# Another written-out order for five passes, and one instruction for the copy of the keys out of PSUM

## The chip, the cores and the metric

The kernel runs on one core of a Trainium2 chip. The time is the device time of one launch in microseconds; the median of three runs is given. One execution was also profiled; all rows below come from it.

## The reference

The program is a chunked attention followed by a two-layer network on its result, `x`:

```
# q, k, v: (4, 8, 768, 64); mem_k, mem_v: (4, 8, 8, 64)
for c in range(768 // 32):                       # chunks of 32 queries
    keys = concat(mem_k, k[..., c0 - 16 : c0 + 32 + 8])   # cut at both ends
    a = softmax(q[..., c0 : c0 + 32] @ keys.T / 8)
    out[..., c0 : c0 + 32] = a @ concat(mem_v, v[same rows])
x = out as (3072 tokens, 512)
h = x @ w_in                                     # w_in: (512, 2048)
g = h + sin(alpha * h) ** 2 / (alpha + 1e-9)
result = g @ w_out                               # w_out: (2048, 512), result float32
```

## The kernel before

**Tiling.** Each of the four batches has 768 tokens. Attention takes 96 queries at a time against 128 key rows (a window of the keys with the 8 memory keys in it), so a batch has 8 blocks `j`, numbered 0 to 7; the first batch is cut by pairs of heads and halves instead. The first matrix product of a batch makes 16 tiles `ft` of 128 features by 768 tokens, in two halves of 384; each half is four matmuls (L426), so a tile is eight matmuls and takes two of PSUM's eight banks. The second product is 6 x 16 matmuls of 512 columns per batch (L464).

**Passes.** The opening pass prepares constants and does the attention of batch 0. Pass `i` (0 to 3) then does both matrix products of batch `i` and, between the matmuls of the second one, the attention of batch `i + 1`. So passes 0, 1 and 2 hold attention, and pass 3 only products. In a pass, TensorE first works through a dense stretch of L426 tiles and then through L464 with the attention strewn in.

**A tile's way.** TensorE makes it (L426); ScalarE takes the sine into `u` (L441); one of ScalarE (L446), VectorE or GpSimd (both L449) squares it; VectorE does `gT = s2 * inv_alpha + hT` out of PSUM (L453) and thereby frees the two banks. With eight banks four tiles can be open; the fifth tile opened needs the first one finished.

**What sets the order.** Nothing is scheduled automatically (`manual_schedule`): the program order of each engine is the order in which a string of words is carried out, one string per pass, and the waits follow from the data. PSUM banks are handed out by `Banks`, always those that were given back longest ago. The words, by their first letter:

- `b`, `h`: first and second half of a tile in L426; `h` also puts the tile's sine on ScalarE.
- `q5A`, `q5V`, `q5P`: the square of tile 5, on ScalarE, VectorE or GpSimd. `g5`: the finishing of tile 5 on VectorE.
- `o`, `f7`: register the second product; take the next seven of its matmuls. At a group's last matmul comes the copy out of PSUM (L471, engine by `e`) and the store.
- `s24`: scores and exponentials of blocks 2 and 4 (L387, L401). `v4`: their values (L416) and the division on VectorE (L355, L356), giving `x_blk`.
- `t4`, `T4`: turn a block on TensorE (L368) and copy it into `xT` (L371), by VectorE (`t`) or ScalarE (`T`). `c4`: turn it by a DMA transpose that SyncE issues (L635).
- `k2`, `l2`: turn the keys or queries of head pair 2 into PSUM (L276). `K2A`, `L2A`: copy them out (`put_k` L287 and L293, `put_q` L301).
- `a4A`: round a loaded piece to bf16 (L655); 0 to 3 are keys, 4 to 7 queries.
- `W`: a one-element activation whose purpose is the table load ahead of sines (`Ws`) or exponentials (`We`).
- `V`, `U`, `I`, `R`, `d`: loads that GpSimd issues (values, `w_out`, `w_in`, rows of keys and queries, others). `X`, `Z`, `c` and the stores go through SyncE. `H` and `m` place memory values; `C` are constants.
- `y`, `z`: matmuls of zeros (128 and 512 columns) that only keep TensorE at work in the opening.

**The copy of the keys.** `kT` holds the keys of a head pair in windows that overlap. `put_k` copies the turned keys out of PSUM in two instructions: one (L287, ScalarE or VectorE by the word) for the seven inner windows of 96 columns, and one (L293, always VectorE) for the two ends of 48. It runs eight times, four in the opening and four in pass 0.

## Time and profile before

| | before |
|---|---|
| median of three runs | 214.72 us (214.53 to 214.74) |
| profiled execution, first to last instruction | 213.2 us |
| opening, to the first L426 | 24.67 us |
| pass 0 | 24.67 to 75.12 |
| pass 1 | 75.12 to 121.70 |
| pass 2 | 121.70 to 167.77 |
| pass 3 | 167.77 to 213.2 |

The profile gives no time of its own for the profiled execution beyond its span; the median of the runs lies 1.5 us above that span, and what lies around the span is not profiled. How to read the rows: "line engine operation out<-in shapes xcount", with the idle time before a row and what ended it in brackets. `L426` is line 426 of the kernel before. Matmuls overlap each other, so a wait of TensorE shorter than a matmul does not show as idle time; it shows when a stretch takes longer than its count of matmuls at the undisturbed rate.

### The profile page before, as it was taken

Reading aid. Unit: us, or ns where it says so; the run is one execution under the profiler, and the core shown is the slowest. Engines: PE = TensorE matmul, PEld = TensorE weight load, DVE = VectorE, ACT = ScalarE, POOL = GpSimd, SP = SyncE. Lnnn points to the kernel's source line nnn. Section 1 sums busy time; section 2 is a strip of 40 time slices with the busy share of each in tenths; the row PEclk is TensorE's granted clock in tenths of the full one; section 3 lists DMA queues with packets and bytes.
Section 4 is the critical chain, followed back from the end, with each engine's and each line's share of the span. In section 5 each row is a group of like instructions: output and inputs, shape, how many; then the busy total and the mean of one; then the engine's idle time right before and its main releaser. Section 6 shows DMA issues by size and latency. Waiting matters only on the chain.

```text
span 213.2 us, 4576 instructions
## 1 busy us (share of the span) xinstructions
PE 205.2 (96%) x1772; PEld 118.0 (55%) x1772; DVE 140.1 (66%) x218; ACT 143.4 (67%) x229; POOL 100.9 (47%) x142
## 2 busy tenths in 40 slices
PE   7898999999999999999999999999999999999994
PEld 7366665665455556555555555554555465654453
DVE  4797788999452749976766659897247187865010
ACT  2598888976848469968837199877756189891110
POOL 8998606599597297109795048664000022200000
PEclk9999999999999999999999999999999999999999
DMA  5999999999999999999999259979944400000312
GB/s 167 323 155 134 208 209 203 205 147 177 130 165 163 166 119 133 111 136 148 143 167 180 68 125 131 143 149 131 131 105 102 141 0 0 5 0 0 148 52 98
DMA packets 95853, 27.82 MB, mean 130 GB/s; under 512 B 84808, under 2 KB 92376, under 8 KB 95832
## 3 DMA queue, kind: packets, MB, share of 16 engines
q0 software_dynamic: 69152, 13.64, 88.1%
q1 hardware_dynamic: 25720, 12.68, 28.7%
q10 hardware_dynamic: 960, 1.21, 1.7%
q8 instruction: 14, 0.23, 0.5%
q14 instruction: 7, 0.06, 0.1%
HBM read 29.66 MB, written 6.29 MB: 169 GB/s over the span
## 4 chain that ended last, share of the span: by engine, by line
PE 73%; DVE 10%; POOL 5%; DMA 4%; ACT 3%; issue 3%; DVEq 0%; POOLq 0%; ACTq 0%
PE ps L464 38%; PE ps L426 29%; DMA vw<-in_v_dram 4%; DVE gT L453 3%; PE ps L416 3%; DVE s L449 3%; PE ps L387 2%; ACT u L441 2%; DVE x_blk L356 2%; ACT s L446 2%; PE ps L368 1%; POOL s L449 1%; POOL vw L172 1%; DVE kT L287 1%; DVE rinv L355 0%
## 5 line engine op out<-in xcount | busy, mean ns | idle before, releaser
L464 PE MATMUL ps<-w_out_sb,gT 128*128 128x512 bf16 (+1 forms) x400 | 89.1, 371 | 0.0
L426 PE MATMUL ps<-xT,w_in_sb 128*128 128x384 bf16 x512 | 86.0, 326 | 0.6 <-DVE gT L453 0.2
L453 DVE SCALAR_TENSOR_TENSOR gT<-s,inv_alpha,ps 128x768 bf16<-128x768 f32 x64 | 63.1, 1012 | 12.3 <-ACT s L446 5.3
L426 PEld LDWEIGHTS <-w_in_sb 128*128 128x128 bf16 x512 | 49.7, 98 | 35.5 <-issue 2.3
L441 ACT ACTIVATE u<-ps,alpha_sb 128x768 f32<-128x768 f32 x64 | 56.7, 895 | 17.1 <-PE ps L426 14.7
L464 PEld LDWEIGHTS <-gT 128*128 128x128 bf16 x400 | 37.1, 98 | 37.2 <-DVE gT L453 0.2
L449 POOL TENSOR_TENSOR s<-u 128x768 f32<-128x768 f32 x11 | 17.2, 1569 | 67.2 <-ACT u L441 56.5
L401 ACT ACTIVATE pt<-ps,biasm 128x256 bf16<-128x256 f32 x72 | 27.2, 489 | 10.5 <-PE ps L387 10.5
L471 DVE COPY o_sb<-ps 128x512 f32<-128x512 f32 (+1 forms) x15 | 10.0, 669 | 27.4 <-PE ps L464 25.5
L449 DVE TENSOR_TENSOR s<-u 128x768 f32<-128x768 f32 x23 | 21.9, 953 | 7.8 <-ACT u L441 7.8
L446 ACT ACTIVATE s<-u 128x768 f32<-128x768 f32 x30 | 25.0, 841 | 0.5
L356 DVE TENSOR_TENSOR x_blk<-ps,rinv 96x512 bf16<-96x512 f32 x32 | 22.0, 687 | 1.1
L471 ACT COPY o_sb<-ps 128x512 f32<-128x512 f32 (+1 forms) x10 | 5.7, 573 | 21.6 <-PE ps L464 21.6
L355 DVE RECIPROCAL rinv<-ps 96x8 f32<-96x8 f32 x32 | 6.4, 199 | 13.3 <-PE ps L416 12.7
L172 POOL DMA_DIRECT2D vw<-in_v_dram x13 | 11.8, 908 | 6.5 <-PE ps L368 5.6
L179 POOL DMA_DIRECT2D vw<-in_v_dram x13 | 13.3, 1021 | 1.6 <-DMA vw<-in_v_dram 1.6
L238 POOL DMA_DIRECT2D kst<-in_k_dram x16 | 13.0, 812 | 1.7 <-DMA vw<-in_v_dram 1.3
L232 POOL DMA_DIRECT2D kst<-in_k_dram x16 | 11.1, 693 | 2.3 <-DMA vw<-in_v_dram 1.4
L245 POOL DMA_DIRECT2D q_bf<-in_q_dram x12 | 10.7, 905 | 0.0
L371 ACT COPY xT<-ps 128x384 bf16<-128x384 bf16 x10 | 4.9, 498 | 8.4 <-PE ps L368 8.4
L416 PEld LDWEIGHTS <-pt 128*128 128x128 bf16 x192 | 8.2, 97 | 4.2 <-ACT pt L401 0.3
L416 PE MATMUL ps<-vw,pt 128*128 128x65 bf16 x192 | 8.9, 193 | 0.0
(84 smaller groups left out, 140.3 us busy)
## 6 DMA issues: line engine op xcount, KB each, us to landing
out_dram<-o_sb SPq DMA_DIRECT2D x23, 256.0 KB, 2.2
q_bf<-in_q_dram POOLq DMA_DIRECT2D x12, 128.0 KB, 7.2
kq_f<-in_k_dram SPq DMA_DIRECT2D x3, 384.0 KB, 5.9
kq_f<-in_q_dram ACTq DMA_DIRECT2D x3, 384.0 KB, 8.6
w_in_sb<-in_moe_w_in_dram POOLq DMA_DIRECT2D x1, 1152.0 KB, 13.1
vw<-in_v_dram POOLq DMA_DIRECT2D x7, 128.0 KB, 8.0
vw<-in_v_dram POOLq DMA_DIRECT2D x8, 112.0 KB, 8.3
kst<-in_k_dram POOLq DMA_DIRECT2D x14, 64.0 KB, 5.2
```

The source lines that it names most:

```text
L172: nc.gpsimd.dma_start(vw[0:64, lo:c1, 0:D], win(vflat, a, n, 64))
L179: nc.gpsimd.dma_start(vw[72:128, c0:hi, 0:D], win(vflat, base + QW * c0 + 48, hi - c0, 56))
L356: nc.vector.tensor_tensor(out=x_blk[:].rearrange("p g e d -> p e g d"), in0=otv[0:QW, :, :, 0:D], in1=rinv[:].unsqueeze(3).to_broadcast([Q ...
L401: nc.scalar.activation(pt[:, 0:H * QW].rearrange("p (g e c) -> p g e c", g=2, e=4)[:, :, :, 32 * m:32 * m + 32], sc[:, :, 0:4 * QW].rearra ...
L416: nc.tensor.matmul(otv[:, e, hp, :], pt[:, QW * i:QW * i + P], vws[b % 2][:, 2 * hp + e, j, 0:D + 1],)
L426: nc.tensor.matmul(t["hT"][:, hf, 0:HALF], w_in_sb[:, kt, P * t["ft"]:P * t["ft"] + P], t["xT"][:, kt, HALF * hf:HALF * hf + HALF], start= ...
L441: nc.scalar.activation(t["u"][:], t["hT"][:, :, 0:HALF], ACTF.Sin, scale=alpha_sb[:, ft:ft + 1])
L446: nc.scalar.activation(s2[:], u[:], ACTF.Square)
L449: e.tensor_tensor(out=s2[:], in0=u[:], in1=u[:], op=ALU.mult)
L453: nc.vector.scalar_tensor_tensor(out=gT[:, ft, :].rearrange("p (e c) -> p e c", e=2), in0=t["s2"][:], scalar=inv_alpha[:, ft:ft + 1], in1= ...
L464: nc.tensor.matmul(o[:, c0:c1], gT[:, ft, P * s:P * s + P], w_out_sb[:, ft, c0:c1], start=(ft == 0), stop=(ft == FT - 1),)
L471: copier(state["engines"][state["o"] % len(state["engines"])])(o_sb[:, c0:c1], o[:, c0:c1])
```

## The change

Two things change. `put_k` becomes one instruction on the engine of the word, which writes all eight windows (768 elements per partition, 8 windows x 2 runs x 48). And the five strings are replaced; they stand at the top of the file now, so that every line below moves down by some 30.

```
 def put_k(b, hp, tb, eng="A"):
     t, bs = tb
-    kT = kTs[b % 2]
+    a = kTs[b % 2][:, hp, 16:848]
     copier(eng)(
-        kT[:, hp, 72:72 + 7 * 104].rearrange("p (s c) -> p s c", c=104)[:, :, 0:96]
-        .rearrange("p s (a r) -> p s a r", r=6),
-        t[:, :, 8:120].rearrange("p r (s a) -> p s a r", a=16),
-    )
-    ends = kT[:, hp, 16:912].rearrange("p (s c) -> p s c", c=112)[:, 0:8:7, 0:48]
-    nc.vector.tensor_copy(
-        ends.rearrange("p s (a r) -> p s a r", r=6),
-        t.rearrange("p r (s a) -> p s a r", a=8)[:, 0:16:15],
+        bass.AP(tensor=a.tensor, offset=a.offset,
+                ap=[list(a.ap[0]), [104, NJ], [56, 2], [6, 8], [1, 6]]),
+        t.rearrange("p r (i u a) -> p i u a r", u=2, a=8),
     )
     banks.give(bs)

 # the opening
-'y1 y1 y1 Ci y1 a4A We y1 Cb a1A y1 y2 y1 y1 dq068 Cl y1 Cm y1 Cf z1 z1 eVA z1 eVA a0A Ck m0 '
-'Cz z1 dk068 Cp V024 z1 z1 V002 z1 a2V V068 z1 z1 Cv l0 z1 a5V z1 L0A k1 k0 z1 k2 l1 K1A V046 '
-'K0A a6V L1A s00 s10 s11 K2V l2 k3 L2V K3A s01 v11 dm l3 L3A v10 s20 v01 s30 v00 s31 v30 s21 '
-'v31 z1 T01 v20 T30 I02 Cs T00 v21 t10 T20 t31 z1 t11 I27 t21 Ws '
+'We a4A y1 y1 Ci y1 a0A y1 Cb Ck y1 Cf y1 y1 z1 dk068 eVA Cp y1 y1 Cm y2 Cl Cz z1 a1V eVA dq068 z1 '
+'V024 m0 V002 l0 L0V k0 a5A k1 a6P y1 l1 K1A K0V L1A a2V V068 z1 s10 s00 k2 l2 l3 K2V L2A Cv L3V s11 '
+'s01 v10 k3 v11 K3A s30 v01 s31 v00 s20 V046 v30 s21 T00 v31 z1 v20 T30 T01 Cs I02 v21 T20 Ws z1 t10 '
+'t31 t11 I27 dm t21 '
 # pass 0
-'o8 b0 h0 I7g q0V U69 U12 b1 h1 dq108 q1A b4 h4 b3 g0 h3 b6 g1 dk108 q4V g4 q3A b2 h2 h6 b5 h5 '
-'Ufg g3 b7 q2V U01 U56 q6P h7 g2 q5A b10 U24 q7P g6 h10 b9 q10A g5 h9 U45 b8 h8 g7 g10 q8A q9V '
-'V158 b11 h11 g9 b13 g8 h13 l0 l2 l3 L0A L2A q13P k2 q11V Ube b15 U9b g11 Uef g13 K2V h15 b12 '
-'q15V h12 q12A b14 g15 f7 h14 V125 k1 k0 g12 l1 K1V k3 L1V L3A q14V K3A K0A V102 dy f9 g14 s61 '
-'f16 m1 s70 s3 f13 v0 f3 v6 Z2 c6 f6 v3 f5 s542 T3 f10 T0 v4 f6 v2 f2 v1 c4 c2 f7 v7 f1 T1 f3 '
-'v5 Ws T7 f8 t5 '
+'b0 h0 U01 b1 I7g h1 b3 q1A U12 o8 q0V b4 h4 dk108 g0 h3 g1 dq108 b6 q4V b2 q3A h2 h6 g4 b5 h5 g3 U45 '
+'Ufg q2V b7 q6P h7 g2 q5A U24 U69 q7P b10 g6 h10 b9 U56 g5 q10A h9 g7 g10 b8 h8 q9V Ube q8P g9 b11 g8 '
+'h11 b13 h13 q11V l0 l2 L0A L2A V102 q13A l3 g11 k2 U9b K2A b15 g13 h15 q15V b12 h12 f3 b14 Uef q12A '
+'g15 h14 f4 k1 V125 g12 l1 k0 L1V k3 V158 L3A K3A K0A K1V q14V g14 f9 m1 s61 f16 s07 s3 dy Z2 f15 v6 '
+'v0 f8 v3 We c6 f4 s542 f2 t3 f11 v4 f2 v2 f1 t0 v1 c2 Ws f10 t1 v7 f5 v5 c4 T7 f6 t5 '
 # pass 1
-'b0 o1 h0 b3 R2 q0V h3 b1 Ws q3A g0 g3 h1 q1V b2 R4 h2 q2A b5 h5 b4 h4 Ws g1 g2 q5V g5 b6 q4A '
-'h6 R8 Ws g4 b8 q6A g6 h8 R1 b9 q8V h9 b7 q9A g8 h7 R3 V378 b11 h11 V226 b10 g9 R4 h10 V202 '
-'V268 q7V Ws q10A f2 X8 q11A g7 f8 b12 h12 g10 g11 b14 h14 q12P g12 b13 h13 q13A g13 q14A f7 '
-'X6 Z3 b15 g14 h15 f7 eV We s24 q15V f6 g15 f7 s05 s1 f1 m2 f14 v4 v1 f6 v0 f1 v2 f2 c4 f6 s63 '
-'s7 t1 f4 c2 v6 T0 f4 v3 f4 v7 c7 v5 t3 f17 t5 T6 '
+'b0 h0 b3 q0V h3 o1 b1 q3A g0 h1 R1 R4 g3 q1V b2 h2 q2A b5 h5 b4 h4 g1 g2 q5V b6 q4A h6 R8 R3 R2 g5 '
+'g4 q6A b8 h8 b9 h9 g6 q8V b7 q9A h7 b11 g8 g9 h11 V378 V202 q7V R4 b10 h10 V268 f3 q10A V226 g7 X6 '
+'q11P X8 f5 g10 b12 h12 b14 Z3 g11 q12V h14 b13 eV h13 g12 q13V f8 b15 g13 q14A g14 h15 f9 q15V s24 '
+'f5 g15 f7 s150 m2 f7 We v4 f10 v1 v0 v2 f8 s63 f6 c4 s7 t0 f6 c2 v3 T1 v6 f1 v7 c7 f3 v5 f13 T3 f5 '
+'T5 We T6 '
 # pass 2
-'b3 R16 H3 Ws b0 h0 h3 b5 h5 Ws b1 q5A q0V g0 q3P R6 g3 X4 h1 Ws q1A b2 h2 X4 g5 g1 b4 h4 b6 '
-'q4A q2V h6 X2 g2 b7 h7 b9 h9 X1 g4 X1 q6V b8 g6 X2 eV o1 h8 q7P g7 q8A b11 h11 q11A q9P b10 '
-'g9 g8 h10 b13 g11 h13 q10V g10 b14 h14 b12 q13P V357 V305 h12 g13 q12V q14A f8 eAV b15 g12 '
-'h15 f6 g14 q15V s24 f16 g15 f2 s103 f9 v4 v0 f3 f2 c4 v3 f2 c3 v2 f1 c2 f6 c0 s675 f10 v1 f4 '
-'c1 Ws f1 v7 v5 c7 v6 f2 c6 c5 f24 '
+'b3 Ws R16 b0 h0 h3 b5 h5 b1 X4 H3 q0V q5A g0 h1 q3P q1A g3 b2 h2 b4 g5 R6 X2 h4 eV g1 q2V X4 X1 b6 '
+'b7 q4A h6 X2 g2 h7 g4 b9 q7P q6V h9 q9P b8 h8 q8A g6 b11 g7 h11 q11A g9 b10 h10 o1 b13 X1 g8 eAV g11 '
+'q10V h13 b14 g10 V305 b12 q13A h14 h12 g13 q14A f4 b15 h15 q15A q12A g14 f17 V357 g12 s24 g15 f11 '
+'s103 f11 v4 v0 c4 f5 c0 v3 v2 f6 c2 s675 c3 f9 We We v1 c1 f6 v7 c7 v6 c6 v5 c5 f27 '
 # pass 3
-'b2 h2 q2V b0 h0 b4 q0A g2 h4 b3 h3 g0 o2 b1 h1 Ws q3P b6 q4V q1A h6 g4 b8 h8 g3 b5 g1 q6A h5 '
-'q5A b7 g6 h7 b11 q8P g8 h11 b10 g5 q7V h10 q10A q11P b9 h9 q9A g7 g11 b12 h12 b15 g10 q12A '
-'h15 g9 g12 b13 h13 b14 q15A h14 g15 q14A q13V g14 g13 '
+'b2 h2 b0 h0 q2V g2 q0A b4 h4 b3 h3 g0 b1 h1 b6 q4V q1P q3A o2 g4 h6 b8 g3 h8 q6A b5 g1 h5 b7 g6 q8P '
+'q5A g8 g5 h7 b11 h11 b10 q7V h10 q10A q11P b9 h9 g7 q9A g11 b12 h12 g10 q12A g9 b15 h15 b13 h13 b14 '
+'q15P h14 g12 q14A q13V g14 g13 g15 '
```

The counts of products, scores, values, sines and stores are the same in both. The zero matmuls fall from 48 of 128 and 14 of 512 columns to 48 and 6; the one-element activations from 13 to 9.

More of the change, by code (lines that the diff above doesn't have):

```diff
@@ L18 @@
 ALU = mybir.AluOpType
+WORDS = (
+    (
[4 rows of a table added]
+    ),
+    (
[5 rows of a table added]
+    ),
+    (
[5 rows of a table added]
+    ),
+    (
[4 rows of a table added]
+    ),
+    (
[3 rows of a table added]
+    ),
+)
 class Feed:
@@ L824 @@
     stage.tile = first
-    stage.run((
[4 rows of a table removed]
-    ))
-    for i, words in enumerate(((
[6 rows of a table removed]
-    ),(
[5 rows of a table removed]
-    ),(
[5 rows of a table removed]
-    ),(
[3 rows of a table removed]
-    ))):
+    stage.run(WORDS[0])
+    for i, words in enumerate(WORDS[1:]):
         stage = Stage(i, stage.nx).run(words)
```

## The prediction

> **What bounds the kernel now.** I read the first part of the page, then TensorE in order of time, the chain of waits, and the dense stretches by windows.
>
> ```profile
> PE 205.2 (96%) x1772; PEld 118.0 (55%) x1772; DVE 140.1 (66%) x218; ACT 143.4 (67%) x229; POOL 100.9 (47%) x142
> ```
>
> TensorE is busy for 205.2 of 213.2 us and no other engine above 67%. An order can only win TensorE's waits, the opening and the tail. The tail stays: the last string ends with the same 112 L464 matmuls. First the opening:
>
> ```profile
> 1.21 4.45 PE L694 MATMUL ps<-zeros 128*128 128x128 bf16 x40 [1.21 <-DVE tiny L731]
> ...
> 22.06 0.41 PE L346 MATMUL ps<-vw,pt 128*128 128x65 bf16 x8 [0.17 <-DMA vw<-in_v_dram]
> ...
> 24.67 5.53 PE L426 MATMUL ps<-xT,w_in_sb 128*128 128x384 bf16 x33
> ```
>
> Network work begins at 24.67. Until then TensorE pads with zeros; what it waits for last is the load of the last values (`V046`). Behind it stand two products and two divisions of 0.20 + 0.69 us on VectorE, then the last turns. The waits after that, by the chain of waits and by two windows (TensorE, busy and count):
>
> ```profile
> 75.28 10.44 PE ps L426 x64
> ...
> 168.68 8.62 PE ps L426 x52
> ```
> ```profile
> 121.70:141.83 20.13, 19.98 (x125) 11.71 (x123) 16.19 (x18) 17.99 (x24) 11.62 (x10) 1.00 1.26 134
> 75.12:90.99 15.87, 15.86 (x100) 9.30 (x98) 13.20 (x15) 14.14 (x20) 9.57 (x11) 1.00 1.70 124
> 24.67:41.99 17.32, 17.26 (x108) 10.07 (x105) 14.30 (x18) 15.62 (x19) 6.86 (x7) 1.00 1.23 207
> 167.77:189.20 21.43, 21.12 (x129) 12.45 (x128) 16.21 (x17) 18.05 (x23) 4.46 (x3) 1.00 0.08 28
> ```
>
> 64 undisturbed L426 take 10.44 us, 0.163 each. The dense stretches hold 15, 12, 13 and 16 tiles of eight: 19.58, 15.66, 16.96 and 20.88 us without a wait. So they lose 0.55 (pass 2), 0.21 (pass 1), 0.36 (pass 0) and 0.55 (pass 3), 1.7 us in all, though nearly none of it shows as idle time. Pass 0 loses perhaps 0.9 more where keys and queries are copied. That is all there is to win behind the opening, and a new order can also lose.
>
> **The change part by part.** *The copy.*
>
> ```profile
> L301 ACT COPY qT<-ps 128x768 bf16<-128x768 bf16 x6 | 4.7, 808 | 0.9 <-PE ps L276 0.9
> ...
> L287 ACT COPY kT<-ps 128x672 bf16<-128x672 bf16 x5 | 3.4, 734 | 0.2 <-PE ps L276 0.2
> ...
> L287 DVE COPY kT<-ps 128x672 bf16<-128x672 bf16 x3 | 2.5, 849 | 0.0
> ...
> L293 DVE COPY kT<-ps 128x96 bf16<-128x96 bf16 x8 | 1.9, 252 | 0.8 <-ACT kT L287 0.7
> ...
> L301 DVE COPY qT<-ps 128x768 bf16<-128x768 bf16 x2 | 1.9, 952 | 0.2 <-PE ps L276 0.2
> ```
>
> 768 elements took 0.81 (ScalarE) and 0.95 us (VectorE) for queries; I take these for the keys. ScalarE pays 5 x 0.07, VectorE 3 x 0.10, and VectorE saves 8 x 0.25: 1.7 us of VectorE. It counts only where VectorE's copy ends a wait, below.
>
> *Opening, 0.0.* Loads of values keep their sequence (`V024 V002 V068 V046`), and `v20 v21` still end it. What is new stands in GpSimd's queue: the cast `a6P`, ahead of `V068` and `V046`.
>
> ```profile
> 9.21 1.82 POOL L179 DMA_DIRECT2D vw<-in_v_dram  x1
> 11.03 0.83 POOL L172 DMA_DIRECT2D vw<-in_v_dram  x1
> ...
> 14.26 0.86 POOL L179 DMA_DIRECT2D vw<-in_v_dram  x1
> ```
> ```profile
> 9.38 1.22 DVE L188 COPY vw<-memv_st 8x4096 bf16<-8x4096 bf16 x1
> ...
> 12.82 0.99 DVE L655 CAST q_bf<-kq_f 128x768 bf16<-128x768 f32 x1
> ```
>
> The piece that `a6P` casts was cast at 12.82, so `a6P` cannot start much earlier, while `V068` was issued at 11.03. A GpSimd cast of 768 isn't shown; GpSimd's L449 on two inputs took 1.57 (quoted below), its plain copy is shorter. The last issue then ends near 18, not 15.1. It used to wait almost seven microseconds to land, at about 22: the transfers queue, so I take the delay as hidden (0). Ends: -0.2, and +2.9 if none is hidden. The first issue above took 1.82 instead of 0.85 while VectorE ran L188. The Trainium skill, DMA: Bandwidth & Descriptors, on software descriptor generation, says that VectorE can lock GpSimd out of writing descriptors; by it the sum would be 0 to +1, and the row agrees.
>
> *Pass 0, -0.1.* Tiles 0 to 8 of the stretch keep their squares and banks, hence its 0.36. Later `q8A q13P` become `q8P q13A`:
>
> ```profile
> 41.99 1.30 PE L276 MATMUL ps<-ident,q_bf 128*64 128x128 bf16 x36
> ...
> 53.16 0.51 PE L387 MATMUL ps<-qT,kT 64*128 64x96 bf16 x16 [0.20 <-DVE kT L293]
> ```
> ```profile
> L453 DVE SCALAR_TENSOR_TENSOR gT<-s,inv_alpha,ps 128x768 bf16<-128x768 f32 x64 | 63.1, 1012 | 12.3 <-ACT s L446 5.3 <-POOL s L449 4.5
> ...
> L446 ACT ACTIVATE s<-u 128x768 f32<-128x768 f32 x30 | 25.0, 841 | 0.5
> ...
> L449 POOL TENSOR_TENSOR s<-u 128x768 f32<-128x768 f32 x11 | 17.2, 1569 | 67.2 <-ACT u L441 56.5 <-issue 10.6
> ```
>
> The GpSimd square is 1.57 - 0.84 = 0.7 longer; ScalarE's queue gives half back, so `l3`, which needs tile 8's banks, comes 0.3 later. Against it the wait at 53.16 (0.20, behind an L293 that no longer exists) goes, and `K2A` replaces `K2V`. -0.2 if all of the wait goes, +0.2 if the GpSimd square runs long; I take -0.1.
>
> *Pass 1, +0.2.* The scores came in three groups (16, 24, 24 matmuls); `s63 f6 c4 s7` splits one.
>
> ```profile
> 101.47 0.51 PE L387 MATMUL ps<-qT,kT 64*128 64x96 bf16 x16
> 101.91 2.98 PE L464 MATMUL ps<-w_out_sb,gT 128*128 128x512 bf16 x13
> 104.83 0.68 PE L387 MATMUL ps<-qT,kT 64*128 64x96 bf16 x24
> 105.44 3.41 PE L464 MATMUL ps<-w_out_sb,gT 128*128 128x512 bf16 x15
> ```
> ```profile
> 162.33 5.61 PE ps L464 x26
> ```
>
> 16 take 0.44 to the next start, 24 take 0.61: eight cost 0.17 and each group 0.10 beside them. The 13 L464 before a group take 2.92, at 0.216 (the 26 of the last fence) 2.81: 0.11 on the way in. A fourth group costs +0.2. Its dense stretch has the same chain of VectorE instructions, so its 0.21 stays.
>
> *Pass 2, +0.55.* Here is the dearest edit. Pass 1 ended `t3 f17 t5 T6`, now `f5 T5 We T6`: the copy for block 5 moves from VectorE to ScalarE, ahead of the table load for the sine.
>
> ```profile
> 121.90 0.48 ACT L371 COPY xT<-ps 128x384 bf16<-128x384 bf16 x1 [4.76 <-PE ps L368]
> 122.40 1.28 ACT L707 ACT_TABLE_LOAD   x1
> ...
> 123.90 1.69 ACT L441 ACTIVATE u<-ps,alpha_sb 128x768 f32<-128x768 f32 x2
> ```
> ```profile
> 124.84 0.96 DVE L449 TENSOR_TENSOR s<-u 128x768 f32<-128x768 f32 x1 [2.32 <-ACT u L441]
> 125.90 1.01 DVE L453 SCALAR_TENSOR_TENSOR gT<-s,inv_alpha,ps 128x768 bf16<-128x768 f32 x1
> 127.23 3.06 DVE L453 SCALAR_TENSOR_TENSOR gT<-s,inv_alpha,ps 128x768 bf16<-128x768 f32 x3 [0.32 <-POOL s L449]
> ```
>
> ScalarE goes from the copy to the load to the first sine without a pause, and VectorE from there to the first finishing (ends 126.91), for which the fifth tile waits. `T5` can start 0.17 earlier than `T6` did (one turn of TensorE), takes 0.43 to 0.48, and `We` 0.08: the first sine comes 0.35 later, the fifth tile too. The finishings behind it keep their order and run back to back, so nothing gives it back. Then `b6 b7 q4A h6 h7` interleaves two tiles; sine 7 and with it `q7P`, `q9P` come some 0.6 later, and VectorE already waited for those squares. Ends: +0.35 (none of this) and +0.8 (nearly all of it less what the shift covers); I take +0.55.
>
> *Pass 3, -0.2.*
>
> ```profile
> 167.77 0.81 PE L426 MATMUL ps<-xT,w_in_sb 128*128 128x384 bf16 x4
> ```
> ```profile
> L635 SPq DMA_TRANSPOSE xT<-x_blk x3: 1207/1249/1887, 162.9 to 166.2; - x3
> ```
> ```profile
> 179.24 0.65 PE L426 MATMUL ps<-xT,w_in_sb 128*128 128x384 bf16 x3
> 180.11 1.14 PE L426 MATMUL ps<-xT,w_in_sb 128*128 128x384 bf16 x6 [0.22 <-DVE gT L453]
> ```
>
> Four matmuls, 0.65, begin at 167.77, and the chain's 52 only at 168.68: 0.26 of wait, with no releaser named. The last of the three DMA transposes there (`c5`) starts at 166.2 and takes up to 1.9; I hold it for the cause. Now 27 instead of 26 L464 and no product stand between the last value product and pass 3, and fewer stores ahead of `c7 c6 c5`: the wait goes. `q1A` and `q3P` change sides (`q3A q1P`); then tile 5 waits for `g3` by 0.2 to 0.4, but tile 11 (three matmuls, 0.49, then 0.38 of wait to 180.11, for `g6` behind ScalarE's `q6A`) waits that much less. +0.05.
>
> Sum: 0.0 - 0.1 + 0.2 + 0.55 - 0.2 = +0.45 on the span of 213.24, 213.7. The median of the runs lies 1.48 above the span; I take this as unchanged: 214.72 + 0.45 = **215.2 us**.
>
> **The rivals.** *Pass 2 absorbs its delay.* In pass 2 the fifth tile's 0.35 merely replaces the 0.55 that this stretch lost later, if VectorE and GpSimd catch up by the thirteenth tile. For it: VectorE had three pauses for GpSimd there. Against: they lie behind the same late sines. Then +0.45 - 0.6 = -0.15: 214.6, not slower.
>
> *VectorE's relief pays.* If the waits of pass 0 at the copies, some 0.9, end with VectorE's copies, all go, and pass 2's delay is absorbed too: -0.9 + 0.2 - 0.25 = -0.95, 213.8. It decides where the last of `K3A K0A K1V` is done before the ninth matmul of `f9`. For it: the row at 53.16. Against: the copies now queue on ScalarE.
>
> *The late issue of the values shows.* If `V046` lands late because `a6P` holds its issue, the first L426 moves with it: +1.0, 216.2; up to +2.9. It decides when the last issue ends later than about 19.5 (22 less some 2.5). Against: seven microseconds from issue to landing.
>
> *The clock.* The 40 zero matmuls took 4.45 us, 0.11 each, against 0.06 at the later rate: TensorE starts at half speed. Now 16 stand ahead of a wait for `Ck`, and eight long ones are gone. If the opening left TensorE slow at the first tiles, 3.4 us of them would take twice as long, +1.7: 216.9. The Trainium skill, TensorE: Matmul & The Clock Gate, Part 1, says that an idle window of about 3.4 us throttles the clock. I count no gap of TensorE above 2 us after that wait.
>
> *The copy isn't what it says*: with five dimensions it could be slower than 0.95; each 0.1 moves only the 0.2 of pass 0. No case of its own.
>
> **How the numbers follow.** Forecast 0.45, with its own range 214.8 to 215.8; absorbed 0.20; relief 0.20; late values 0.11; clock 0.04. A measurement of this kernel tells 0.2%, 0.43 us, from no change; the forecast lies at that edge. Faster: 0.19 of relief and 0.06 of absorbed, 0.25. Within: 0.17 of the forecast, 0.14 of absorbed, 0.01 of relief, 0.32. Slower: the rest, 0.43. The range goes from the relief to the late values, 213.8 to 216.2; it leaves the clock, the worse late values and a margin outside.
>
> **What would show it.** Opening: first L426 within 0.3 of 24.67. Pass 1: four groups of scores. Pass 2: from its first L426 to the first sine 2.5 us or more (2.2 before), and fifteen tiles over 20.3. Pass 3: no wait for the DMA. I am wrong if the first L426 comes earlier by half a microsecond, or pass 2's tiles take under 20.

## The result and the profile after

| | before | changed |
|---|---|---|
| median of six runs | 214.73 us (214.50 to 214.94) | 217.44 us (216.53 to 218.26) |
| ratio (95% interval) | | 1.0124 (1.0101 to 1.0148) |
| span of the profiled execution | 213.2 | 215.0 (its own time 217.12) |

The change makes the kernel 1.2% slower, 2.7 us. The changed kernel's lines lie some 30 further on: L426 is L456, L464 is L494, L449 is L479, L453 is L483, L276 is L311, L219 is L254. The forecast's first row has its answer in the page of the profile after:

```profile
PE 204.4 (95%) x1764; PEld 117.7 (55%) x1764; DVE 138.7 (65%) x211; ACT 143.0 (67%) x223; POOL 100.5 (47%) x143
```

TensorE does eight matmuls less and is busy a little less, in a span that is 1.8 us longer: only waits were added. Windows from one pass's first L456 to the next one's show where (start:end, length, then busy time and count by engine):

```profile
25.11:76.06 50.95, 50.07 (x472) 28.61 (x470) 35.85 (x52) 37.61 (x61) 31.04 (x38) 1.00 1.61 175
76.06:122.86 46.80, 46.79 (x376) 25.77 (x374) 35.05 (x49) 31.44 (x52) 28.11 (x37) 1.00 1.43 137
122.86:169.28 46.42, 46.10 (x356) 25.15 (x354) 27.73 (x39) 36.73 (x61) 14.09 (x13) 1.00 1.14 120
169.28:214.99 45.71, 42.04 (x241) 23.31 (x239) 22.42 (x24) 22.16 (x28) 5.91 (x4) 1.00 0.13 49
```

Against before that is +0.44 for the opening (25.11 for 24.67), +0.50 for pass 0, +0.22 for pass 1, +0.35 for pass 2 and +0.24 for pass 3: 1.75 us. The medians lie 2.7 apart, 0.96 more. The time of a run is longer than its span, by 1.78 us in the kernel before (median of 35 runs) and by 2.14 in the changed one. So the profiled execution of before took some 215.0 us, 0.3 above its median; that of the changed kernel, 217.12, lies 0.3 below its own. The last 0.36 lie outside the span, where no profile shows them: their cause stays open. One execution of open_ck (217.56) and one of p2_f2 (217.96) below were in the chip's slower state and are left out of every median and ratio here.

**Opening.** TensorE in order of time, for the changed kernel:

```profile
1.20 1.89 PE L724 MATMUL ps<-zeros 128*128 128x128 bf16 x16 [1.20 <-DVE tiny L761]
6.03 0.27 PE L810 MATMUL ps<-ident,memv_st 16*128 16x16 bf16 x4 [2.94 <-DVE memv_st L806]
6.23 1.46 PE L724 MATMUL ps<-zeros 128*128 128x128 bf16 x12
...
11.04 0.53 PE L311 MATMUL ps<-ident,q_bf 128*64 128x128 bf16 x12
...
25.11 1.14 PE L456 MATMUL ps<-xT,w_in_sb 128*128 128x384 bf16 x6
```

After 16 zero matmuls TensorE waits 2.94 us for the memory keys; the twelve that follow take 1.46 us, which is still half the rate that TensorE reaches later, and the first turn of queries comes at 11.04 (before: 9.71).

**The dense stretches** of passes 2, 1, 0 and 3, as in the prediction:

```profile
122.86:142.99 20.13, 19.94 (x125) 11.71 (x123) 16.01 (x18) 18.76 (x25) 14.09 (x13) 1.00 1.44 129
76.06:91.89 15.83, 15.82 (x100) 9.32 (x98) 13.20 (x15) 14.04 (x17) 10.10 (x13) 1.00 1.80 134
25.11:43.01 17.90, 17.42 (x108) 10.16 (x106) 14.43 (x18) 15.03 (x19) 8.57 (x8) 1.00 1.24 206
169.28:190.95 21.67, 21.12 (x130) 12.44 (x128) 16.21 (x17) 18.02 (x22) 4.77 (x4) 1.00 0.09 30
```

Pass 2 takes 20.13, to the hundredth what it took before; pass 0 takes 17.90 for 17.32, pass 3 21.67 for 21.43.

**Pass 0.** GpSimd in order of time, first in the kernel before, then in the changed one:

```profile
35.40 0.77 POOL L219 DMA_DIRECT2D w_out_sb<-in_moe_w_out_dram  x1
36.26 1.46 POOL L449 TENSOR_TENSOR s<-u 128x768 f32<-128x768 f32 x1
```
```profile
35.95 1.55 POOL L254 DMA_DIRECT2D w_out_sb<-in_moe_w_out_dram  x2
37.51 1.49 POOL L479 TENSOR_TENSOR s<-u 128x768 f32<-128x768 f32 x1
...
40.94 2.23 POOL L479 TENSOR_TENSOR s<-u 128x768 f32<-128x768 f32 x1 [0.67 <-ACT u L471]
```

Two loads instead of one stand ahead of the second square, so it starts 12.40 us after the pass's first L456 and not 11.59. The third (`q8P`) takes 2.23.

**Pass 2 and 3.** ScalarE at the start of pass 2, then TensorE inside it and at the start of pass 3:

```profile
122.89 0.48 ACT L401 COPY xT<-ps 128x384 bf16<-128x384 bf16 x1 [0.78 <-PE ps L398]
...
123.84 1.28 ACT L737 ACT_TABLE_LOAD   x1
...
125.25 2.62 ACT L471 ACTIVATE u<-ps,alpha_sb 128x768 f32<-128x768 f32 x3
```
```profile
154.84 0.65 PE L446 MATMUL ps<-vw,pt 128*128 128x65 bf16 x16
155.33 1.24 PE L494 MATMUL ps<-w_out_sb,gT 128*128 128x512 bf16 x5
156.41 0.64 PE L446 MATMUL ps<-vw,pt 128*128 128x65 bf16 x16
157.17 1.46 PE L494 MATMUL ps<-w_out_sb,gT 128*128 128x512 bf16 x6
...
169.28 0.81 PE L456 MATMUL ps<-xT,w_in_sb 128*128 128x384 bf16 x4
170.47 1.78 PE L456 MATMUL ps<-xT,w_in_sb 128*128 128x384 bf16 x10 [0.38 <-DMA xT<-x_blk]
```

The first sine starts 2.39 us after the pass's first matmul, where it was 2.20. Sixteen L446 take 0.49 to the next start at 154.84 and 0.76 at 156.41: 0.27 of waiting for a bank that a division on VectorE holds, new in this order. And pass 3's wait for the DMA transpose is not gone but longer: 1.19 from 169.28 for four matmuls of 0.163, so 0.54 instead of 0.26. SyncE's queue ahead of it, first before, then in the changed kernel:

```profile
160.83 0.34 SPq L474 DMA_DIRECT2D out_dram<-o_sb  x1
161.66 5.76 SPq L635 DMA_TRANSPOSE xT<-x_blk  x4
```
```profile
163.87 1.44 SPq L504 DMA_DIRECT2D out_dram<-o_sb  x1
165.40 3.81 SPq L665 DMA_TRANSPOSE xT<-x_blk  x3
```

The last three transposes are `c7 c6 c5`. The division that `c7` needs had ended at 164.10, but a store of 1.44 us held the queue until 165.3, and the three follow each other from there.

### The profile page after: what moved, and what is told of

Its sections match the earlier page's. It is cut to its first block, busy times and chain, and to the rows that moved or that the text cites. A ratio compares the mean times of both kernels' runs of the same rounds, so it can differ in the third digit from the quotient of the medians.

```text
span 215.0 us, 4554 instructions
## 1 busy us (share of the span) xinstructions
PE 204.4 (95%) x1764; PEld 117.7 (55%) x1764; DVE 138.7 (65%) x211; ACT 143.0 (67%) x223; POOL 100.5 (47%) x143
## 3 DMA queue, kind: packets, MB, share of 16 engines
q10 hardware_dynamic: 960, 1.21, 1.7%
## 4 chain that ended last, share of the span: by engine, by line
PE 67%; issue 10%; DVE 9%; ACT 4%; POOL 4%; DMA 3%; SPq 1%; ACTq 0%; DVEq 0%; POOLq 0%
PE ps L494 31%; PE ps L456 28%; DVE gT L483 4%; DVE x_blk L386 2%; PE ps L417 2%; DMA memk_f<-in_mem_k_dram 2%; POOL vw L230 2%; POOL s L479 2%; DVE s L479 2%; PE ps L311 2%; PE ps L724 1%; PE ps L446 1%; DMA xT<-x_blk 1%; ACT pt L364 1%; DVE rinv L385 1%
## 5 line engine op out<-in xcount | busy, mean ns | idle before, releaser
L494 PE MATMUL ps<-w_out_sb,gT 128*128 128x512 bf16 (+1 forms) x400 | 89.0, 371 | 0.1
L456 PE MATMUL ps<-xT,w_in_sb 128*128 128x384 bf16 x512 | 86.0, 326 | 1.1 <-DVE gT L483 0.5
L483 DVE SCALAR_TENSOR_TENSOR gT<-s,inv_alpha,ps 128x768 bf16<-128x768 f32 x64 | 63.1, 1012 | 11.4 <-ACT s L476 6.3
L456 PEld LDWEIGHTS <-w_in_sb 128*128 128x128 bf16 x512 | 49.6, 98 | 35.9 <-issue 2.8
L494 PEld LDWEIGHTS <-gT 128*128 128x128 bf16 x400 | 37.3, 98 | 37.5 <-issue 0.2
L479 POOL TENSOR_TENSOR s<-u 128x768 f32<-128x768 f32 x11 | 17.8, 1623 | 70.9 <-ACT u L471 57.8
L479 DVE TENSOR_TENSOR s<-u 128x768 f32<-128x768 f32 x23 | 22.5, 979 | 10.1 <-ACT u L471 10.0
L267 POOL DMA_DIRECT2D kst<-in_k_dram x16 | 11.7, 731 | 4.3 <-DMA vw<-in_v_dram 3.3
L273 POOL DMA_DIRECT2D kst<-in_k_dram x16 | 11.6, 726 | 2.5 <-DMA vw<-in_v_dram 2.4
L401 ACT COPY xT<-ps 128x384 bf16<-128x384 bf16 x9 | 4.2, 475 | 9.7 <-PE ps L398 9.6
L446 PEld LDWEIGHTS <-pt 128*128 128x128 bf16 x192 | 8.0, 97 | 3.2
L446 PE MATMUL ps<-vw,pt 128*128 128x65 bf16 x192 | 8.6, 193 | 0.0
```

Of the source, the lines that this page charges most:

```text
L446: nc.tensor.matmul(otv[:, e, hp, :], pt[:, QW * i:QW * i + P], vws[b % 2][:, 2 * hp + e, j, 0:D + 1],)
L456: nc.tensor.matmul(t["hT"][:, hf, 0:HALF], w_in_sb[:, kt, P * t["ft"]:P * t["ft"] + P], t["xT"][:, kt, HALF * hf:HALF * hf + HALF], start= ...
L479: e.tensor_tensor(out=s2[:], in0=u[:], in1=u[:], op=ALU.mult)
L483: nc.vector.scalar_tensor_tensor(out=gT[:, ft, :].rearrange("p (e c) -> p e c", e=2), in0=t["s2"][:], scalar=inv_alpha[:, ft:ft + 1], in1= ...
L494: nc.tensor.matmul(o[:, c0:c1], gT[:, ft, P * s:P * s + P], w_out_sb[:, ft, c0:c1], start=(ft == 0), stop=(ft == FT - 1),)
```

## The experiments

All kernels have the new copy of the keys. "Old" strings are those before the change, "new" ones the changed kernel's. Lines lie one to three further on than in the changed kernel (L458 for L456). Ratios are to the kernel before, run beside them, with 95% intervals.

### Which part costs what: copy_only, open_new, p0_new, p123_new

```diff
 strings:     opening  pass 0  pass 1  pass 2  pass 3
 copy_only    old      old     old     old     old
 open_new     new      old     old     old     old
 p0_new       old      new     old     old     old
 p123_new     old      old     new     new     new
```

> The kernel before with the new one-instruction copy of the keys alone, all five strings as before. Theory A (the copy is harmless, the orders make the loss): eight L293 of 0.25 us leave VectorE, the wait of 0.27 us ahead of the first scores of pass 0 (53.16 in the profile before) shrinks, and the median is 0 to 0.4 us under the kernel before. Rival B (the copy itself, with its five dimensions, is the loss): each copy takes well over 0.8 us on ScalarE or 0.95 us on VectorE, and the median is 0.5 us or more above the kernel before.

> New copy, the changed kernel's string for the opening, the four other strings as before. Theory A (each string costs what its own stretch shows in the two profiles): first L426 at 25.1 instead of 24.67, median 0.3 to 0.5 us above the kernel with the new copy alone. Theory C (the loss that the two profiles do not show, 2.7 us between the medians against 1.8 between the profiled spans, and the wide spread of the changed kernel, 216.5 to 218.3, come from the opening, whose loads land at another time in each execution): 1 to 1.5 us above, with executions spread over more than 1 us.

> New copy, the changed kernel's string for pass 0, the four other strings as before. Theory A: pass 0 is 0.5 us longer (GpSimd issues two loads of w_out ahead of its second square, and the third square on GpSimd takes 2.2 us where ScalarE took 0.84), so the median is about 0.5 us above the kernel with the new copy alone, with a spread like before, under 0.5 us. Theory D (the spread and the missing 0.9 us come from pass 0, where loads and squares share GpSimd): 1 to 1.5 us above, spread over more than 1 us.

> New copy, the changed kernel's strings for passes 1, 2 and 3, the opening and pass 0 as before. Theory A: +0.22 (a fourth group of scores in pass 1), +0.35 (end of pass 2: a wait of the second product's bank for a division on VectorE, 0.29) and +0.25 (a longer wait for the DMA transpose at the start of pass 3), in all 0.8 us above the kernel with the new copy alone, spread under 0.5 us. Rival: under 0.4, then most of the loss comes from the opening and pass 0.

Measured, before at 214.80:

| | before | copy_only | open_new | p0_new | p123_new |
|---|---|---|---|---|---|
| median, us | 214.80 | 214.38 | 215.54 | 215.18 | 215.31 |
| ratio | | 0.9985 (0.9967, 1.0004) | 1.0037 (1.0018, 1.0056) | 1.0023 (1.0002, 1.0043) | 1.0026 (1.0008, 1.0045) |
| first L426 | 24.67 | 24.48 | 24.99 | 24.07 | 23.87 |
| pass 0 | 50.45 | 50.16 | 50.16 | 50.94 | 50.15 |
| pass 1 | 46.58 | 46.58 | 46.58 | 46.62 | 46.84 |
| pass 2 | 46.07 | 46.06 | 46.07 | 46.07 | 46.56 |
| pass 3 | 45.47 | 45.22 | 45.66 | 45.45 | 45.46 |

In these five profiles a pass's length repeats to 0.05 us wherever its string and the copy are the same, so the parts can be read separately. Pass 3 is the exception: its old string takes 45.22 to 45.66, its new one 45.46 to 45.71 (changed kernel), so an effect of 0.24 there is hardly clear of the spread. The copy gains 0.29 in pass 0: the wait of 0.27 behind L293 is gone. Theory A holds for it; as a whole kernel the gain, 0.42, is not clear of the noise. Against copy_only the new opening costs 1.16, pass 0 0.80, passes 1 to 3 0.93. With the copy's -0.42 that adds up to 2.47 of the 2.71 measured.

The opening costs 1.16, as Theory C had it in size, although the two profiles showed 0.44. The old opening with the new copy is read in nine profiles of the kernels in this section: the first L426 comes at 23.68 to 24.63, on average at 24.10. The 24.67 of the profile before is later than all of them: there the last values landed at 21.93 and TensorE waited for them. It also has the old copy, whose share of this was not separated. The new opening's come at 24.99 and 25.11, 0.95 later on average. Some 0.6 of that is steady: the first L426 follows the first exponential by 10.2 to 10.5 in the nine profiles, and by 10.88 and 10.81 in the two, because the third division comes 1.39 behind the second instead of 0.84 to 0.93. The other 0.35 is less sure: the first exponential itself comes at 13.50 to 14.45 in the nine, and 14.11 and 14.30 in the two lie inside that range. The spread of a kernel's executions tells nothing: copy_only's executions reach from 214.12 to 215.81, those of before, in 35 runs, from 214.26 to 216.03.

### Pass 0: p0_u69, p0_q8A, old_u69, best_u24

```diff
 p0_u69 (p0_new with)
-... q5A U24 U69 q7P b10 ...
+... q5A U24 q7P U69 b10 ...
 p0_q8A (p0_new with)
-... q9V Ube q8P g9 ...
+... q9V Ube q8A g9 ...
 old_u69 (copy_only with)
-o8 b0 h0 I7g q0V U69 U12 ... q5A b10 U24 q7P ...
+o8 b0 h0 I7g q0V U12 ... q5A b10 U24 U69 q7P ...
 best_u24 (copy_only with)
-... b10 U24 q7P ...
+... b10 q7P U24 ...
```

> Run p0_new with one word of pass 0 moved: U69 (a load of w_out that GpSimd issues, 0.78 us) behind q7P instead of ahead of it. Theory G (a DMA issue on GpSimd ahead of a square holds up the finishings behind it): the wait of 0.34 us at the eleventh tile (39.05 in p0_new) goes to 0.1, pass 0 takes 50.6 to 50.7 instead of 50.94. Rival (the fifth to eighth squares are bound elsewhere): 50.9.

> Run p0_new with the square of tile 8 on ScalarE, as it was, instead of GpSimd (q8A for q8P). Theory H (GpSimd takes 2.2 us for it beside VectorE, ScalarE 0.84, and tile 8's banks are needed by the turns of the keys and queries): the waits of 0.3 and 0.58 us ahead of the turns (41.96, 43.21 in p0_new) shrink by 0.5 or more, pass 0 takes 50.4 instead of 50.94. Rival (ScalarE's queue gives it back, as the prediction took for half of it): 50.7 to 50.9.

> Run copy_only (the old orders) with one word of pass 0 moved the other way: U69, one load of w_out that GpSimd issues, from the start of the pass to just ahead of q7P, where the changed kernel has it. Theory G (a DMA issue of 0.78 us ahead of GpSimd's square delays the finishings and, through the banks, the tiles and the turns): pass 0 takes 50.4 to 50.9 instead of 50.16, median 0.3 to 0.7 over copy_only. Rival (it only hurts in the changed kernel's order of squares): 50.16 to 50.25.

> Run copy_only with one word of pass 0 moved: U24, a load that GpSimd issues, behind the square q7P instead of ahead of it. Theory G (an issue ahead of a square on GpSimd costs what the square comes later): GpSimd's second square starts about 0.1 earlier only, since in copy_only it waited 0.09 us for its sine behind the issue anyway, so the wait of 0.11 us at 37.81 shrinks or goes, and pass 0 takes 50.05 to 50.15; median as copy_only, 0.1 to 0.5 under the kernel before. Rival: 50.16 to 50.3, because the load lands later.

Medians and ratios: p0_u69 214.68, 1.0015 (0.9993, 1.0038); p0_q8A 215.08, 1.0030 (1.0010, 1.0051); old_u69 214.91, 1.0010 (0.9990, 1.0029); best_u24 214.70, 0.9994 (0.9968, 1.0020). Pass 0 by windows, for copy_only, p0_new, p0_u69, p0_q8A and old_u69:

```profile
24.48:74.64 50.16, 49.98 (x473) 28.60 (x471) 35.34 (x49) 38.05 (x62) 30.42 (x38) 1.00 1.67 175
```
```profile
24.07:75.01 50.94, 50.07 (x473) 28.60 (x471) 35.55 (x51) 37.79 (x61) 31.34 (x38) 1.00 1.63 174
```
```profile
23.76:74.00 50.24, 49.85 (x473) 28.54 (x471) 35.47 (x51) 37.71 (x61) 30.37 (x38) 1.00 1.68 177
```
```profile
23.96:74.59 50.63, 50.07 (x473) 28.61 (x471) 35.46 (x51) 38.44 (x62) 28.68 (x36) 1.00 1.70 175
```
```profile
24.05:74.67 50.62, 49.81 (x467) 28.59 (x470) 35.39 (x49) 38.06 (x62) 31.61 (x38) 1.00 1.67 176
```

One word, one load of 0.78 us, makes 0.70 of the new pass 0's 0.78, and put into the old order it costs 0.46, both by the length of pass 0 in the profiles: the whole kernels' medians don't resolve it (p0_u69 1.0015 and p0_new 1.0023, intervals that overlap). Theory G holds, and it is stronger than I wrote, for a reason that GpSimd's and VectorE's rows show, first in p0_new, then in p0_u69:

```profile
39.90 2.21 POOL L481 TENSOR_TENSOR s<-u 128x768 f32<-128x768 f32 x1 [0.69 <-ACT u L473]
```
```profile
39.84 0.95 DVE L481 TENSOR_TENSOR s<-u 128x768 f32<-128x768 f32 x1
```
```profile
39.60 1.50 POOL L481 TENSOR_TENSOR s<-u 128x768 f32<-128x768 f32 x1 [0.68 <-ACT u L473]
```
```profile
38.83 0.95 DVE L481 TENSOR_TENSOR s<-u 128x768 f32<-128x768 f32 x1
```

The late second square holds up VectorE's finishings by 0.62, so VectorE's next square comes to lie on top of GpSimd's third one, which then takes 2.21 instead of 1.50; tile 8's finishing and the turns behind it come later again. The Trainium skill, SBUF — State Buffer, section "SBUF: two separate sides", says that VectorE and GpSimd share a pair of ports under an exclusive lock, and that whichever instruction starts first keeps it to its end. The rows agree: VectorE's square starts 0.06 ahead and takes its usual 0.95, GpSimd's takes 0.71 more. The old order has it too: 2.19 in old_u69, and 1.82 in copy_only, where VectorE's square stands 0.45 ahead.

p0_q8A (50.63) gives back 0.31 of the 0.54 expected: Theory H is half right, since the wait at the eleventh tile stays. best_u24 gave nothing readable: its profiled execution lost 0.35 to a load of `w_in` (27.75) that has no part in the edit, and its median is that of the kernel before within the interval.

### The opening: open_ck, open_nz, open_s20, open_k3, hyb_newset, hyb_newrest

```diff
 open_ck (open_new with)
-... Cb Ck y1 Cf ... V024 m0 ...
+... Cb y1 Cf ... V024 Ck m0 ...
 open_nz (open_new with)
-Ck y1 Cf y1 y1 z1 dk068 eVA Cp y1 y1 Cm y2 Cl Cz z1 a1V eVA dq068 z1 V024
+Ck Cf dk068 eVA Cp Cm Cl Cz a1V eVA dq068 V024
 open_s20 (open_new with)
-... K3A s30 v01 s31 v00 s20 V046 v30 s21 T00 v31 z1 v20 ...
+... K3A s20 v01 s21 v00 s30 V046 v20 s31 T00 v21 z1 v30 ...
 open_k3 (open_new with)
-... L3V s11 s01 v10 k3 v11 K3A s30 ...
+... L3V k3 K3A s11 s01 v10 v11 s30 ...
 hyb_newset:  new up to "a2V V068 z1", then Cv k2 V046 and the old words from "s00 s10 s11"
 hyb_newrest: old up to "a6V L1A", then the new words from "s10 s00"
```

> Run open_new with one word of the opening moved: Ck (the memory keys, whose turn TensorE waits for from 2.9 to 6.0 us behind only 16 zero matmuls) goes behind the other constants and zeros, just ahead of m0. Theory E (the wait lets TensorE fall back to half rate: its zero matmuls of 128 columns then take 0.105 us each up to 9.6 us where the kernel before has 0.06 from 5.7 us on, and the first turn comes at 10.9 to 11.0 instead of 8.8 to 9.7): zero matmuls at 0.06 from about 5.5 us, first turn at 9.7 or earlier, first L426 at 24.3 or earlier, median 0.8 us or more under open_new (215.54), about that of copy_only (214.38). Rival F (the new opening is bound by its loads and by ScalarE's and VectorE's sequence of copies and divisions, whatever TensorE does): first L426 within 0.3 of 25.0, median within 0.4 of open_new.

> Run open_new without the 28 zero matmuls of 128 and the zero matmuls of 512 columns between Ck and the first turn (the work that counts stays). Theory J (the slow zero matmuls hold up the first turn, and with it the first exponential): first turn at 8.0 to 9.0 instead of 10.85, first exponential at 13.7 or earlier instead of 14.1, median 0.4 or more under open_new. Rival K (the first exponential waits for casts and copies on ScalarE and VectorE behind their loads): first turn earlier, first exponential at 14.0 or later, median within 0.3 of open_new or above it, since TensorE is then slow in the first turns.

> Run open_new with head pairs 2 and 3 exchanged in the second half of the opening (s20 v01 s21 v00 s30 ... for s30 v01 s31 v00 s20 ...), so that the score behind the copy K3A is one of pair 2, whose keys were copied earlier. Theory I (in open_new the score s30 waits 0.61 us on TensorE for K3A, which stands on ScalarE behind two exponentials, and VectorE's divisions, back to back in the kernel before, lose 0.5 us there): from the first exponential to the first L426 10.2 to 10.4 us instead of 10.88, median 0.4 to 0.6 under open_new (215.54), so 214.9 to 215.1. Rival (the values that land last, or ScalarE's eight exponentials, bind the same stretch anyway): 10.8 or more, median 215.4 or more.

> Run open_new with k3 and K3A (turn and copy of head pair 3's keys) ahead of the scores s11 s01 instead of behind them and v10. Theory I, second form (the score s30 waits 0.61 us on TensorE for this copy, and ScalarE stands idle 0.44 us for that score): the wait goes, from the first exponential to the first L426 10.3 to 10.5 us instead of 10.88. Rival (ScalarE's sequence is full, so a copy put earlier only moves the exponentials of s11 and s01, and the divisions, later by as much): 10.8 or more.

> Opening made of the changed kernel's words up to the first score and of the old words from there on; new copy, old passes. Theory L (each half of the opening holds what the profiles show: 0.45 us up to the first exponential, 0.69 behind it): first exponential near 14.2, then 10.2 us to the first L426, median about 0.45 over copy_only (0.3 to 0.6). Rival M (the loss comes with the loads that the changed first half issues late, whatever follows): 0.9 or more over copy_only.

> Opening made of the old words up to the first score and of the changed kernel's from there on; new copy, old passes. Theory L: first exponential near 13.7, then 10.9 us to the first L426, because the third head pair's copy K3A stands behind two more exponentials on ScalarE and TensorE's next score waits for it; median 0.5 to 0.8 over copy_only. Rival M: within 0.2 of copy_only.

| | first turn | first exponential | first L426 | between | median | ratio |
|---|---|---|---|---|---|---|
| copy_only | 8.83 | 14.29 | 24.48 | 10.19 | 214.38 | 0.9985 |
| open_new | 10.85 | 14.11 | 24.99 | 10.88 | 215.54 | 1.0037 |
| open_ck | 9.78 | 14.66 | 25.57 | 10.91 | 215.47 | 1.0051 (1.0026, 1.0075) |
| open_nz | 8.13 | 12.72 | 23.99 | 11.27 | 215.23 | 1.0015 (0.9996, 1.0034) |
| open_s20 | 10.80 | 14.16 | 25.59 | 11.43 | 215.84 | 1.0066 (1.0039, 1.0093) |
| open_k3 | 10.80 | 14.05 | 25.18 | 11.13 | 215.38 | 1.0043 (1.0013, 1.0073) |
| hyb_newset | 10.03 | 15.30 | 26.28 | 10.98 | 216.97 | 1.0109 (1.0089, 1.0129) |
| hyb_newrest | 9.69 | 14.06 | 24.79 | 10.73 | 216.00 | 1.0055 (1.0033, 1.0077) |

open_ck's median lies where Rival F has it, its first L458 is later than either theory has it, and it didn't test Theory E: with `Ck` moved, VectorE stands at the cast `a1V`, whose load is late, ahead of the memory keys. TensorE waits 1.01 us at 6.99 and 1.82 us for their turn at 9.57, and is slow after that, here by the clock too (the column behind POOL's count):

```profile
9.50:12.00 2.50, 2.42 (x42) 2.23 (x43) 2.06 (x6) 0.88 (x2) 0.66 (x1) 0.50 1.40 222
```

open_nz is the clean test. Its TensorE, and a later place of the same kernel:

```profile
5.80 0.27 PE L812 MATMUL ps<-ident,memv_st 16*128 16x16 bf16 x4 [2.71 <-DVE memv_st L808]
...
8.13 0.85 PE L313 MATMUL ps<-ident,q_bf 128*64 128x128 bf16 x12
...
54.18 2.10 PE L496 MATMUL ps<-w_out_sb,gT 128*128 128x512 bf16 x9 [1.10 <-DMA w_out_sb<-in_moe_w_out_dram]
```

Without the zeros the first turn comes 2.7 earlier, the first exponential 1.4, the first L458 1.0, though the turns themselves run at half rate (0.85 for twelve instead of 0.53). Theory J holds: the slow zeros hold up the new opening. Without them it still ends only where the old opening, which has zeros, ends on average (23.99 and 24.10). And the kernel gains only 0.3 to 0.4 (215.23 beside 214.91 for before, 215.54 beside 214.80): in this execution pass 0 takes 51.47, because at 54.18 it waits 1.10 for a load of `w_out` that GpSimd issued in sequence. An earlier start runs into the loads.

Behind the first exponential, the score that waits for `K3A` is real, here in open_new's TensorE, ScalarE and VectorE:

```profile
18.62 0.34 PE L359 MATMUL ps<-qT,kT 64*128 64x96 bf16 x8 [0.36 <-ACT kT L324]
```
```profile
19.01 3.21 ACT L366 ACTIVATE pt<-ps 128x768 bf16<-128x768 f32 x4 [0.44 <-PE ps L359]
```
```profile
19.36 0.20 DVE L387 RECIPROCAL rinv<-ps 96x8 f32<-96x8 f32 x1 [0.48 <-PE ps L378]
```

Still, both mends failed. Exchanging the pairs (open_s20) put a wait of 0.9 behind a division (its profiled execution was also 2.2 over its median, with 0.9 us lost in pass 0 to a load), and taking `K3A` forward (open_k3) delays the first division:

```profile
18.00 0.20 DVE L387 RECIPROCAL rinv<-ps 96x8 f32<-96x8 f32 x1 [0.59 <-PE ps L378]
```

It stood at 17.12 in open_new. From 18.00 the eight divisions run back to back, 0.84 each, to 24.79. So this half is bound by VectorE's eight divisions, 6.7 us, behind the first exponentials; an order can only start them early and keep them together, as the old one does (17.11 to 24.09 in copy_only), and the rival was right. The two hybrids don't add up: hyb_newrest shows 0.54 behind the first exponential, near the 0.69 of Theory L, but hyb_newset starts the exponentials at 15.30, later than either parent: its string has the turn `k2` ahead of the first score, and TensorE waits 2.28 us there for the cast `a2V` on VectorE. The granted clock then falls to 0.61 (15 to 18 us), and the first division follows the first exponential by 3.77 us instead of 2.82 (copy_only). So it is no clean test of the first half. hyb_newset's 2.3 us over the kernel before are its opening's. hyb_newrest's 1.3 are more than its opening explains: in its profile pass 1, whose string is the old one, takes 47.64 instead of 46.58, first behind a DMA transpose of queries; why it does so there stays open.

### Passes 1 to 3: p123_fix, p2_f2, best_q6

```diff
 p123_fix (p123_new with), pass 1 and pass 2
-... f8 s63 f6 c4 s7 t0 ...
+... f8 s63 s7 f6 c4 t0 ...
-... c0 v3 v2 f6 c2 ... v5 c5 f27
+... c0 v3 f2 v2 f4 c2 ... v5 f12 T5 f15
 p2_f2 (copy_only with the new pass 2, and in it)
-... c0 v3 v2 f6 c2 ...
+... c0 v3 f2 v2 f4 c2 ...
 best_q6 (copy_only with), pass 3
-... b8 h8 g3 b5 g1 q6A h5 ...
+... b8 q6A h8 g3 b5 g1 h5 ...
```

> Run p123_new with three edits, one for each stretch: the scores of block 7 stand directly behind those of 6 and 3 again (three groups instead of four); in pass 2 two matmuls of the second product stand between v3 and v2; block 5 of the last batch is turned on TensorE and copied by ScalarE (T5, 12 matmuls behind v5) instead of by a DMA transpose. Expected if my reading of the stretches holds: pass 1 46.62 instead of 46.84 (0.21 for a group), pass 2 46.3 to 46.4 instead of 46.56 (the wait of 0.28 for a division goes, the extra turn costs 0.17), pass 3 45.1 to 45.2 instead of 45.46 (the wait for the transpose, 0.30, goes); median about 214.7 against 215.31. If the groups and waits are only symptoms, each stretch stays within 0.1.

> Run copy_only with the changed kernel's string for pass 2 alone (pass 1 old, so without T5 T6 at its end), and in it two matmuls of the second product between v3 and v2. Theory N (the loss of pass 2 is the wait of 0.28 us for a division that holds a PSUM bank, not the later sine): pass 2 takes 46.05 to 46.2, and median within 0.2 of copy_only. Rival (the sine's order, the prediction's step): 46.35 to 46.5 still.

> Run copy_only with one word of pass 3 moved: tile 6's square on ScalarE (q6A) stands ahead of tile 8's sine instead of behind it, so that the finishing g6 and the banks that tile 11 waits for 0.39 us come earlier. Expected: the wait at tile 11 shrinks by 0.2 to 0.39, pass 3 45.0 instead of 45.22, median 0.2 to 0.4 under copy_only, if no later tile waits in its place; else pass 3 stays at 45.2.

Passes 1 to 3 by windows, in p123_new and in p123_fix (median 215.36, 1.0032 (1.0009, 1.0055)):

```profile
74.03:120.87 46.84, 46.83 (x377) 25.71 (x374) 35.01 (x49) 31.47 (x52) 27.12 (x36) 1.00 1.48 137
120.87:167.43 46.56, 46.24 (x356) 25.20 (x354) 27.73 (x39) 36.76 (x61) 14.09 (x13) 1.00 1.09 120
167.43:212.89 45.46, 42.04 (x241) 23.32 (x239) 22.41 (x24) 22.18 (x28) 5.91 (x4) 1.00 0.13 48
```
```profile
73.83:121.04 47.21, 46.96 (x376) 25.85 (x374) 35.00 (x49) 31.43 (x52) 28.10 (x36) 1.00 1.45 136
121.04:167.56 46.52, 46.33 (x361) 25.30 (x359) 27.73 (x39) 37.11 (x62) 14.09 (x13) 1.00 1.10 120
167.56:212.81 45.25, 41.88 (x241) 23.38 (x239) 22.41 (x24) 22.16 (x28) 5.91 (x4) 0.99 0.12 47
```

Pass 1 got 0.37 longer, not 0.22 shorter: with three values shortly ahead of them, the 24 scores in one group wait 0.27 for a bank that a division frees, and the next L496 wait 0.31. In the new order the fourth group is the price for that, and the cheaper one. Pass 2, less the 0.17 that a turn on TensorE costs, is 0.21 shorter, but 0.14 of that lies elsewhere: p123_new's 16 scores at 146.92 take 0.59 to the next start for 0.45, which the edit doesn't touch. The wait of 0.28 did go (two groups of eight values take 0.24 each), but most of it came back beside and behind them, 0.13 of it at the next 24 scores, so the stretch gained 0.07. Pass 3 is 0.21 shorter without the wait for the transpose, inside its spread. The turn eats most of that.

p2_f2 misses Theory N: 215.15, 1.0018 (0.9991, 1.0046), is 0.8 over copy_only where N had at most 0.2; its profiled execution is the slow one. So the profiles show where pass 2 loses, behind the dense stretch, where values, scores and divisions pass the banks to each other. That this one wait is the cause was tested and not borne out; some 0.3 of the loss stays open.

best_q6, the attempt at something faster, costs 1.5: 216.20, 1.0086 (1.0055, 1.0117). Its TensorE, VectorE and GpSimd in pass 3:

```profile
185.32 1.95 PE L458 MATMUL ps<-xT,w_in_sb 128*128 128x384 bf16 x11 [1.37 <-DVE gT L485]
```
```profile
181.98 2.17 DVE L481 TENSOR_TENSOR s<-u 128x768 f32<-128x768 f32 x1
```
```profile
181.87 1.47 POOL L481 TENSOR_TENSOR s<-u 128x768 f32<-128x768 f32 x1 [1.78 <-ACT u L473]
```

Tile 8's sine, one place later, delays GpSimd's square `q8P`; everything behind it slips until the two squares meet, this time with GpSimd first: VectorE's takes 2.17 instead of 0.95.

### Two mends in the changed kernel: after_fix

```diff
 after_fix: the changed kernel with the pass 0 of p0_u69 and the opening of open_s20
```

> The changed kernel with two mends: U69 behind q7P in pass 0, and head pairs 2 and 3 exchanged in the opening as in open_s20. If both theories hold and the parts add up: first L426 0.5 earlier than in the changed kernel, pass 0 50.23 instead of 50.95, median 1.1 to 1.3 under the changed kernel, about 216.2, still 1.4 above the kernel before. If the parts don't add up (the passes lean on each other's loads), 216.8 or more.

216.93 us, 1.0100 (1.0072, 1.0127): 2.0 over the kernel before instead of 2.7. Pass 0 takes 50.23, as in p0_u69: that mend carries over whole. The opening's (first L426 at 25.28) doesn't, as in open_s20. No kernel here is clear of noise under the kernel before; copy_only comes nearest.

## Why the prediction was wrong, point by point

- **Opening, 0.0: the step that failed most.** I held the opening to be bound by the landing of the last values, and the whole question to be whether `a6P` delays it. The cast took 0.82 and the last issue ended at 17.12, not near 18; the values landed earlier (20.59 for 21.93), and the opening is 0.95 to 1.16 longer. It is bound by the sequence first turn, first exponential, eight divisions. The new order breaks the row of divisions (0.44 of idle ScalarE and 0.48 of idle VectorE), some 0.6 in every profile; it starts the exponentials some 0.35 later on average, behind slow zeros, which is inside the spread of the old order. The wait for the values that carried my step, 0.17 at 22.06, shows in only one of the nine other profiles of the old opening, and cost even the kernel before less than 0.1: its next division comes 0.93 behind the one before, where 0.84 is the shortest.
- **The clock**, a rival at 0.04, was in part the cause, by another way than I wrote: no tile was slow, but the zeros themselves were, and they stand ahead of the first turn. I had counted no pause above 2 us *after* the wait for `Ck` and not looked at the wait itself (2.94). The count was no safe sign either: in open_ck pauses of 1.01 and 1.82 us were enough for a granted clock of 0.50.
- **Pass 0, -0.1: failed.** The copy's share came out (-0.29, I gave up to -0.2). The order's +0.79 I put at 0.3 for `q8P`. I compared the squares engine by engine but not the loads that GpSimd issues between them, though a moved DMA issue of 0.78 us stood in the order.
- **Pass 1, +0.2: right**, 0.22, size and cause. That the split also saves a longer wait I had not seen.
- **Pass 2, +0.55: direction right, cause wrong.** The table load starts 0.28 later and the sine follows it 0.09 closer, so the first sine is 0.19 later, not 0.35; the dense stretch absorbs that wholly (20.13 twice), as the first rival said. The +0.35 come behind it: 0.28 at the second sixteen L446 and 0.07 at the 24 behind them. Why they don't go with the wait (p123_fix) stays open.
- **Pass 3, -0.2: failed**, +0.24 between the profiles. 27 matmuls of cover instead of 26 did not do: block 5's division ends at 165.77, and `c5`, third behind `c7` and `c6` as before, starts at 168.01. I had written of fewer stores ahead of them, and there is a longer one (1.44). No run took that store away, so this reading isn't tested, and the +0.24 is hardly clear of the pass's spread.
- **From the span to the median.** I took the 1.48 between one profiled span and the median for the work around the span. The runs that have both give 1.78 for before and 2.14 for the changed kernel (medians), so it was not unchanged, by 0.36 us that no profile shows; and the profiled execution of before lay some 0.3 above its own median.

VectorE's relief, the rival at 213.8, got a third of its price: the copy gave 0.29 of the 0.9 in pass 0.
